# The second half of a matmul stage by Strassen's seven products: 1280 of 2304 tokens of the output projection

## The chip, the cores and the metric

The kernel runs on one core of a Trainium2 chip. The metric is device time in microseconds (us), the time of the slowest core, of which there is one here. The engines are TensorE (PE, and PEld for its weight loads), VectorE (DVE), ScalarE (ACT), GpSimd (POOL, unused) and SyncE (SP, which only issues DMAs). PSUM is the memory that TensorE accumulates in, eight banks of 512 float32 a partition; SBUF is the memory that all engines read.

## The reference

A retention layer feeds a gated layer, and that feeds a layer with a leaky activation; 2304 tokens, float32 in and out (the weights come as float64):

```python
a, b = x @ w1, x @ w2                    # x: 2304 x 512 from the attention
x2 = (a * b @ w3) @ w_out                # 512 wide
h = x2 @ w_in                            # 2304 x 2048
g = np.maximum(h, 0) + alpha * np.minimum(h, 0)
out = g @ w_out2                         # 2304 x 2048 times 2048 x 512
```

Only the last line is touched.

## The kernel before

Every product is made from float32 values cut in two: a high part (a cast to fp32r, on ScalarE) and a low part (value minus high part, on VectorE). A product is three passes: high by high, high by low, low by high. So each operand has to be cut before TensorE can read it.

The stages follow one another on TensorE: the retention, a times b, a fold of w3 with w_out, y (x2), h (x2 @ w_in), and out. The h stage is already done with Strassen's seven products, on pairs of token blocks; its g goes to DRAM in tiles of 128 rows x 384 tokens (`gd[c, b]`).

The out stage (line 970) is a list of 48 steps (line 878): for each of six blocks of W = 384 tokens, eight steps j; a step takes two of the 16 chunks of 128 rows of w_out2 (`wbc[2j]`, `wbc[2j+1]`, each high and low). The first 16 steps alternate between blocks 0 and 1, for w_out2 is still being converted from float64 then; after that each block has its eight steps in a row. A step issues 3 chunks of tokens x 2 chunks of rows x 3 passes = 18 matmuls with 512 columns; g is the stationary operand, w_out2 the moving one. Each chunk of 128 tokens has a PSUM bank, which is copied and written out after its step j = 7 (`write`).

Three steps ahead SP loads g (`load_g`, tiles `gr`, three buffers), one step ahead ScalarE and VectorE cut it (`split_g`, tiles `gh` and `gl`, two buffers). The conversion of w_out2 (`Weights`, a step of it at each tick) takes VectorE's time in the early steps.

TensorE, ScalarE and SP run their instructions in the order of the code. VectorE's order is set by a scheduler when the program is built; on the chip each of the four engines works off its own list in order.

Of the kernel before, what the change touches and what calls it, by code (L numbers as in the profile page):

```python
# [7 lines left out]
F32 = mybir.dt.float32  # L8
# [24 lines left out]
def _f32(ap):  # L33
    return ap.bitcast(F32)
# [103 lines left out]
def retention_moe_kernel(ctx: ExitStack, tc, qk, kv, w_out1, w3t, w12, w_in, w_out2, alpha, c_row, c_pair, out):  # L138
    nc = tc.nc

    def pool(stack, name, bufs=1, **kw):
        return stack.enter_context(tc.tile_pool(name=name, bufs=bufs, **kw))
# [634 lines left out]
    py.close()  # L777


    back = pool(ctx, "back", side="right", reuse_waits="tile")  # L780
    pg = ExitStack()
    gp = pool(pg, "gp", side="right", bufs=2, reuse_waits="tile")

    def fetch(q, u):
# [90 lines left out]
            self.from_sum(self.b3, self.u2, 0, 1)  # L875

    NM = W // P
    steps = [(j, b) for j in range(C1) for b in range(2)] + [(j, b) for b in range(2, NB) for j in range(C1)]
    loaded, ready, accs = {}, {}, {}

    def load_g(n):
        if n < len(steps):
            j, b = steps[n]
            t = loaded[n] = gr.tile([P, 2, W], F32, tag="gr", name=f"gr{n}")
            for m in range(2):
                nc.sync.dma_start(out=t[:, m], in_=gd[2 * j + m, b])

    def split_g(n):
        if n < len(steps):
            x = loaded.pop(n)  # L890
            ready[n] = tuple(ghl.tile([P, 2, W], F32R, tag=f"g{m}", name=f"g{m}{n}") for m in "hl")
            split(ready[n][0], ready[n][1], x)

    def write(b, i):
# [70 lines left out]
    flush()  # L965


    pg.close()
    used = 0
    for n, (j, b) in enumerate(steps):  # L970
        if ws.at[3] < len(ws.pieces):
            ws.tick()
            ws.until(n_in + 2 * j + 2)
        load_g(n + 3)
        split_g(n + 1)
        if b not in accs:
            accs[b] = [bank((used + i) % 8, f"o{b}_{i}") for i in range(NM)]
            used += NM
        h, l = ready.pop(n)
        for i in range(NM):  # L980
            ic = slice(i * P, (i + 1) * P)
            for m in range(2):
                wh, wl = wbc[2 * j + m]
                for q, (x, y) in enumerate(((h, wh), (h, wl), (l, wh))):
                    nc.tensor.matmul(accs[b][i], x[:, m, ic], y, start=(j == 0 and m == 0 and q == 0),  # L985
                                     stop=(j == C1 - 1 and m == 1 and q == 2))
            if j == C1 - 1:
                write(b, i)


# [79 lines left out]
```

## Time and profile before

| | us |
|---|---|
| median of 3 runs (lowest to highest) | 812.07 (811.72 to 814.09) |
| the profiled execution | 812.48 |
| its span, from the first to the last instruction | 810.7 |
| TensorE busy | 793.1 |
| VectorE busy | 499.6 |
| ScalarE busy | 349.7 |

The mean granted clock of TensorE is 0.992 of 2.4 GHz. In rows of a timeline a name such as `o<-wb,gh` is the tile written and those read; "[3.12 <-PE o]" says that the engine sat idle for 3.12 us and that TensorE's write of o ended it. Matmuls overlap in the pipeline, so their spacing is read from their starts and not from their durations. DMA issues have a row on SP's queue (SPq).

### The profile page before, as it was taken

The page shows a single profiled execution, that of the slowest core. Times are in us where ns is not written, and L with a number is a line of the kernel's source. Part 1 is how long each engine was busy: PE and PEld are TensorE (multiplying, and loading weights), DVE is VectorE, ACT ScalarE, POOL GpSimd, SP SyncE. Part 2 cuts the span into 40 slices and gives each one's busy share as a digit, 9 for nine tenths or more (in the row PEclk, how much of TensorE's full clock was granted, in tenths as well). Part 3 has the DMA queues.
Part 4 walks back from the last instruction along what each step waited for, and adds up shares of the span by engine and source line. Part 5 has one row for each costly group of instructions (what it writes and reads, how often), then busy time and mean ns, then how long its engine had stood idle before and what let it go on. Part 6 is the DMA issues. An engine that isn't in the chain of part 4 may idle for free.

```text
span 810.7 us, 12667 instructions
## 1 busy us (share of the span) xinstructions
PE 793.1 (98%) x4768; PEld 699.9 (86%) x4768; DVE 499.6 (62%) x895; ACT 349.7 (43%) x648; POOL 0.2 (0%) x4
## 2 busy tenths in 40 slices
PE   7989999999999999999999999999999999999998
PEld 4768888888888988999999999999997888888886
DVE  4786776325467789979752568677889923222222
ACT  3452562232245566655534455455566622222221
POOL 0000000000000000000000000000000000000000
PEclk8989999999999999999999999999999999999999
DMA  9845821371076658999934935325566735344341
GB/s 348 300 142 200 303 112 78 105 280 79 27 229 181 213 184 300 308 375 402 394 129 151 380 116 186 127 98 186 172 212 223 238 98 175 97 138 137 98 135 40
DMA packets 78845, 155.91 MB, mean 192 GB/s; under 512 B 7872, under 2 KB 55488, under 8 KB 78784
## 3 DMA queue, kind: packets, MB, share of 16 engines
q1 hardware_dynamic: 78784, 155.10, 54.5%
q8 instruction: 37, 0.61, 0.3%
q14 instruction: 24, 0.20, 0.1%
HBM read 103.69 MB, written 51.38 MB: 191 GB/s over the span
## 4 chain that ended last, share of the span: by engine, by line
PE 92%; DMA 3%; ACT 2%; DVE 1%; SPq 1%; issue 0%; ACTq 0%
PE ps L179 24%; PE o L985 23%; PE h L824 21%; PE y L757 12%; PE pw L571 5%; PE o L320 2%; DMA kv<-in_kv_dram 2%; PE sc L274 2%; PE o L312 1%; DMA gr<-gd 1%; PE st L288 1%; DVE xs L327 0%; ACT xh L172 0%; PE sc L264 0%; DVE gl L173 0%
## 5 line engine op out<-in xcount | busy, mean ns | idle before, releaser
L179 PE MATMUL ps<-xh,w 128*128 128x512 f32 (+1 forms) x640 | 187.5, 374 | 1.8 <-ACT w L112 1.7
L985 PE MATMUL o<-wb,gh 128*128 128x512 f32 x576 | 177.6, 389 | 1.2 <-ACT gh L172 1.2
L179 PEld LDWEIGHTS ps<-xh,w 128*128 128x128 f32 x640 | 116.9, 190 | 23.7 <-ACT w L112 1.9
L985 PEld LDWEIGHTS o<-wb,gh 128*128 128x128 f32 x576 | 108.0, 188 | 24.0 <-ACT gh L172 1.7
L179 PE MATMUL ps<-xl,w 128*128 128x512 f32 (+1 forms) x320 | 118.8, 371 | 0.0
L985 PE MATMUL o<-wb,gl 128*128 128x512 f32 x288 | 112.3, 390 | 0.5 <-DVE gl L173 0.5
L173 DVE TENSOR_TENSOR gl<-gr,gh 128x768 fp32r<-128x768 f32 x48 | 45.9, 957 | 100.2 <-ACT gh L172 100.0
L757 PE MATMUL y<-yab,wp 128*128 128x384 f32 x576 | 100.0, 334 | 0.0
L757 PEld LDWEIGHTS y<-yab,wp 128*128 128x128 f32 x576 | 99.9, 188 | 0.1
L172 ACT CAST gh<-gr 128x768 fp32r<-128x768 f32 x48 | 40.2, 839 | 116.2 <-PE o L985 111.3
L179 PEld LDWEIGHTS ps<-xl,w 128*128 128x128 f32 x320 | 60.9, 190 | 10.0 <-DVE xl L173 0.3
L985 PEld LDWEIGHTS o<-wb,gl 128*128 128x128 f32 x288 | 54.0, 188 | 12.4 <-DVE gl L173 1.3
L836 DVE SCALAR_TENSOR_TENSOR g<-m,al,g 128x384 f32<-128x384 f32 x48 | 29.7, 618 | 48.2 <-ACT g L835 47.9
L824 PE MATMUL h<-xT,wv 128*128 128x384 f32 x288 | 54.9, 334 | 1.4 <-DVE g L842 1.4
L824 PE MATMUL h<-xT,wu 128*128 128x384 f32 x288 | 55.0, 335 | 0.3 <-ACT h L849 0.3
L108 DVE CUSTOM_DVE_ANT_0 a<-a,b 128x1024 uint16<-128x1024 uint16 x72 | 49.5, 687 | 3.8 <-DVE a L106 0.5
L824 PEld LDWEIGHTS h<-xT,wv 128*128 128x128 f32 x288 | 50.3, 188 | 1.8 <-DVE g L842 1.8
L824 PEld LDWEIGHTS h<-xT,wu 128*128 128x128 f32 x288 | 50.3, 188 | 0.9 <-ACT h L849 0.6
L433 ACT CAST ab<-f 128x512 fp32r<-128x512 f32 (+1 forms) x40 | 23.1, 576 | 64.2 <-DVE f L437 59.8
L437 DVE TENSOR_TENSOR f<-f,ps 128x512 f32<-128x512 f32 (+1 forms) x40 | 25.3, 632 | 35.3 <-PE ps L179 35.0
L103 DVE TENSOR_SCALAR a<-a 128x512 f32<-128x512 f32 x72 | 30.4, 422 | 22.2 <-ACT a L93 21.9
L571 PE MATMUL pw<-wo,w 128*128 128x512 f32 x192 | 43.7, 389 | 0.0
(82 smaller groups left out, 1012.9 us busy)
## 6 DMA issues: line engine op xcount, KB each, us to landing
gd<-g SPq DMA_DIRECT2D x96, 192.0 KB, 1.9
gr<-gd SPq DMA_DIRECT2D x96, 192.0 KB, 2.5
abd<-ab SPq DMA_DIRECT2D x32, 512.0 KB, 3.7
raw<-in_w_out_dram SPq DMA_DIRECT2D x24, 512.0 KB, 4.0
qk<-in_qk_dram SPq DMA_DIRECT2D x16, 576.0 KB, 7.1
yab<-abd SPq DMA_DIRECT2D x24, 384.0 KB, 8.5
kv<-in_kv_dram SPq DMA_DIRECT2D x16, 544.0 KB, 7.9
raw<-in_w_dram SPq DMA_DIRECT2D x16, 512.0 KB, 7.4
```

The costliest lines, as they stand in the source:

```text
L103: nc.vector.tensor_scalar(out=a, in0=a, scalar1=self.LEAST, scalar2=self.MOST, op0=ALU.max, op1=ALU.min)
L108: nc.vector.tensor_tensor(out=a.bitcast(I32), in0=a.bitcast(I32), in1=b, op=ALU.add)
L172: nc.scalar.copy(hi, src)
L173: nc.vector.tensor_tensor(out=lo, in0=src, in1=_f32(hi), op=ALU.subtract)
L179: nc.tensor.matmul(ps, a, bb, start=(n == 0), stop=(n == last))
L433: nc.scalar.copy(t[:, 0], f)
L437: nc.vector.tensor_tensor(out=f, in0=f, in1=pss[1], op=ALU.mult)
L571: nc.tensor.matmul(acc[i], a[:, ic], bb, start=(k == 0 and n == 0), stop=(k == C1 - 1 and n == 2))
L757: nc.tensor.matmul(ys[o], wpc[c][a][:, oc], yab[b, c][:, bb], start=(c == 0 and i == 0), stop=(c == C1 - 1 and i == 2))
L824: nc.tensor.matmul(ps, a[:, x, ks], b[:, y, k], start=(fresh and n == 0), stop=(n == 5), skip_group_check=True)
L836: nc.vector.scalar_tensor_tensor(out=g, in0=r, scalar=neg[:, c:c + 1], in1=g, op0=ALU.mult, op1=ALU.add)
L985: nc.tensor.matmul(accs[b][i], x[:, m, ic], y, start=(j == 0 and m == 0 and q == 0), stop=(j == C1 - 1 and m == 1 and q == 2))
```

## The change

Blocks 0 and 1 (384 tokens) and the first 256 tokens of block 2 stay as they were: 24 steps, the last eight of them with 12 matmuls instead of 18. The other 1280 tokens are five groups of 256. For such a group g, as a matrix of two halves of tokens by two chunks of rows, is multiplied with the 2 x 2 blocks of two chunks of w_out2 (128 rows x 256 columns each) by seven products instead of eight, in the form with 15 sums. A tail step is one j of one group: seven products x three passes = 21 matmuls with 256 columns, into four banks (`q`) that hold two halves each; eight steps make a group.

What is new around it:
- `t_sums`, `rest`: for each j the sums of w_out2's blocks. w0 and w1 add high and low part again, t12 and t34 hold the four sums; `t123` and `t4` take their high parts (ScalarE) and low parts (VectorE). Sixteen pieces; one is issued at each plain step once the conversion of w_out2 is through, what is left after the last plain step.
- `load_two`, `add_two`: for two steps eight loads of 128 x 128 of g into a tile `gs` (three buffers) and four sums of it on VectorE.
- `high_part`, `low_part`: the seven operands of a step cut in two in one instruction each (128 x 896), tiles `go` (three buffers); `high_part(n + 2)` and `low_part(n + 1)` are issued at step n.
- after the last step of a group the four banks are added up on VectorE (one copy on ScalarE) and written with two DMAs.
- the room of `back` (tiles of w_in's operands) is closed before the out stage and used for `gs` and `go`.

```diff
-    steps = [(j, b) for j in range(C1) for b in range(2)] + [(j, b) for b in range(2, NB) for j in range(C1)]
+    PLAIN = ((0, W), (1, W), (2, 256))
+    steps = [(j, *x) for j in range(C1) for x in PLAIN[:2]] + [(j, *PLAIN[2]) for j in range(C1)]
...
+    gs = pool(ctx, "gs", side="right", bufs=3, reuse_waits="tile")
+    go = pool(ctx, "go", side="right", bufs=3, reuse_waits="tile")
...
+        for m, w in enumerate((w0, w1)):
+            h, l = wbc[2 * j + m]
+            nc.vector.tensor_tensor(out=w, in0=_f32(h), in1=_f32(l), op=ALU.add)
+        less(t12[:, :HW], w0[:, HW:], w0[:, :HW])
+        less(t12[:, HW:], w1[:, HW:], t12[:, :HW])
+
+        def rest():
+            t34 = tmp.tile([P, DM], I32, tag="b", name=f"t34_{j}", bufs=2).bitcast(F32)
+            less(t34[:, :HW], w1[:, HW:], w0[:, HW:])
+            less(t34[:, HW:], w1[:, :HW], t12[:, HW:])
...
+            for t, cols, src in places:
+                nc.scalar.copy(t[:, 0, cols], src)
+            for t, cols, src in places:
+                nc.vector.tensor_tensor(out=t[:, 1, cols], in0=src, in1=_f32(t[:, 0, cols]), op=ALU.subtract)
...
+    def load_two(u):
...
+        t = sums_of[u] = gs.tile([P, 2, 7, P], F32, tag="gs", name=f"gs{u}")
+        t0 = T0 + 2 * u // C1 * 256
+        for i in range(2):
+            j = (2 * u + i) % C1
+            for m in range(2):
+                for h in range(2):
+                    b, at = divmod(t0 + h * P, W)
+                    nc.sync.dma_start(out=t[:, i, PLACE[f"A{h + 1}{m + 1}"]],
+                                      in_=gd[2 * j + m, b][:, at:at + P])
...
+        for out, x, y, how in (("S1", "A21", "A22", ALU.add), ("S3", "A11", "A21", ALU.subtract),
+                               ("S2", "S1", "A11", ALU.subtract), ("S4", "A12", "S2", ALU.subtract)):
+            nc.vector.tensor_tensor(out=a[out], in0=a[x], in1=a[y], op=how)
...
+    PRODUCTS = (("A11", "B11", 0, 0), ("S2", "T2", 0, 1), ("S3", "T3", 1, 0), ("S1", "T1", 2, 1), ("A22", "T4", 2, 0),
+                ("A12", "B21", 3, 0), ("S4", "B22", 3, 1))
+
+    ahead = [lambda: load_two(0), lambda: load_two(1), lambda: load_two(2), lambda: add_two(0), lambda: add_two(1),
+             lambda: high_part(0), lambda: (low_part(0), high_part(1))]
...
-    for n, (j, b) in enumerate(steps):
+    for n, (j, b, w) in enumerate(steps):
         if ws.at[3] < len(ws.pieces):
             ws.tick()
             ws.until(n_in + 2 * j + 2)
+        else:
+            t_steps.tick(1)
         load_g(n + 3)
         split_g(n + 1)
+        if n >= len(steps) - len(ahead):
+            ahead.pop(0)()
...
+    t_steps.rest()
+
+    for n in range(n_tail):
...
+        high_part(n + 2)
+        low_part(n + 1)
+        if n % 2:
+            add_two(n // 2 + 2)
+            load_two(n // 2 + 3)
+        x = gops.pop(n)
+        for a, op, k, half in PRODUCTS:
...
+            for i, (y, z) in enumerate(((0, 0), (0, 1), (1, 0))):
+                nc.tensor.matmul(ps, a[:, y], b[z], start=(opens and j == 0 and i == 0),
+                                 stop=(j == C1 - 1 and i == 2), skip_group_check=True)
...
+            elif op == "B22":
+                nc.vector.tensor_tensor(out=ot[:, :DM], in0=e, in1=four[3], op=ALU.add)
+                nc.sync.dma_start(out=out[t0:t0 + P, :], in_=ot[:, :DM])
```

How the engines' lists move is not in the diff. On VectorE, in the kernel before, the place where block 2 ends (gl21 to gl25 are low parts of g for the 22nd to the 26th step, ot2 the copies of finished banks) reads:

```order
L173 TENSOR_TENSOR gl21_7105<-gr21_7051,gh21_7104 128x768
L173 TENSOR_TENSOR gl22_7130<-gr22_7076,gh22_7129 128x768
L173 TENSOR_TENSOR gl23_7155<-gr23_7101,gh23_7154 128x768
L173 TENSOR_TENSOR gl24_7180<-gr24_7126,gh24_7179 128x768
L899 COPY ot2_0_7189<-o2_0_7005 128x512
L899 COPY ot2_2_7207<-o2_2_7007 128x512
L173 TENSOR_TENSOR gl25_7214<-gr25_7151,gh25_7213 128x768
```

There VectorE had one low part a step. In the changed kernel the rows that follow the last plain step's (gs3 are sums of g for the seventh and eighth tail step, t12_7 and t34_7 the last sums of w_out2, go2 the operands of the third tail step) read:

```order
L1042 TENSOR_TENSOR gs3_7367<-gs3_7367 128x2x128
L986 TENSOR_TENSOR t12_7_7317<-w0_7_7315 128x256
L986 TENSOR_TENSOR t34_7_7322<-w1_7_7316,w0_7_7315 128x256
L1042 TENSOR_TENSOR gs3_7367<-gs3_7367 128x2x128
L986 TENSOR_TENSOR t12_7_7317<-w1_7_7316,t12_7_7317 128x256
L1042 TENSOR_TENSOR gs3_7367<-gs3_7367 128x2x128
L986 TENSOR_TENSOR t34_7_7322<-w1_7_7316,t12_7_7317 128x256
L1042 TENSOR_TENSOR gs3_7367<-gs3_7367 128x2x128
L1007 TENSOR_TENSOR t123_7_7325<-t12_7_7317,t123_7_7325 128x512
L1007 TENSOR_TENSOR t123_7_7325<-t34_7_7322,t123_7_7325 128x256
L1007 TENSOR_TENSOR t4_6_7308<-t34_7_7322,t4_6_7308 128x256
L1052 TENSOR_TENSOR go2_7336<-gs1_7114,go2_7336 128x896
```

So the low part of the third tail step stands behind all the sums of w_out2 and behind sums of g for four tail steps later.

ScalarE in the kernel before, about the same place:

```order
L172 CAST gh23_7154<-gr23_7101 128x768
L172 CAST gh24_7179<-gr24_7126 128x768
L897 COPY ot2_1_7198<-o2_1_7006 128x512
L172 CAST gh25_7213<-gr25_7151 128x768
L172 CAST gh26_7241<-gr26_7176 128x768
```

And in the changed kernel, from the high part of the second tail step (go1) past the copy of the last plain bank (ot2_1) to the high part of the third (go2):

```order
L1047 CAST go1_7267<-gs0_7075 128x896
L899 COPY ot2_1_7284<-o2_1_7048 128x512
L1005 CAST t123_5_7290<-t12_5_7261 128x512
L1005 CAST t123_5_7290<-t34_5_7287 128x256
L1005 CAST t4_4_7234<-t34_5_7287 128x256
L1005 CAST t123_6_7307<-t12_6_7299 128x512
L1005 CAST t123_6_7307<-t34_6_7304 128x256
L1005 CAST t4_6_7308<-t34_6_7304 128x256
L1005 CAST t123_7_7325<-t12_7_7317 128x512
L1005 CAST t123_7_7325<-t34_7_7322 128x256
L1005 CAST t4_6_7308<-t34_7_7322 128x256
L1047 CAST go2_7336<-gs1_7114 128x896
```

Nine casts for the last three sets of sums have come between, and each set's source is written on VectorE after the casts of the set before it.

## Rows read from the trace of the kernel before

**Rows 1.** The page: TensorE's busy share, and the chain that ended last.
```profile
PE 793.1 (98%) x4768; PEld 699.9 (86%) x4768; DVE 499.6 (62%) x895; ACT 349.7 (43%) x648; POOL 0.2 (0%) x4
...
PE 92%; DMA 3%; ACT 2%; DVE 1%; SPq 1%; issue 0%; ACTq 0%
```

**Rows 2.** Table by stretches: width, busy time (instructions) by engine, granted clock, DMA.
```profile
core 0: us, PE busy (x) PEld busy (x) DVE busy (x) ACT busy (x) POOL busy (x), PEclk, DMA share, GB/s
...
632.00:652.00 20.00, 20.00 (x90) 16.57 (x89) 17.43 (x29) 11.36 (x19) 0.00 (x0) 1.00 0.64 211
652.00:676.00 24.00, 24.00 (x108) 19.87 (x107) 8.20 (x10) 6.34 (x9) 0.00 (x0) 1.00 0.36 115
676.00:700.00 24.00, 24.00 (x108) 19.87 (x107) 6.39 (x7) 5.03 (x6) 0.00 (x0) 1.00 0.44 139
...
265.00:287.00 22.00, 22.00 (x185) 22.00 (x185) 15.57 (x33) 10.86 (x25) 0.00 (x0) 1.00 0.57 178
```

**Rows 3.** TensorE in order of time, 512 columns: start, duration, what, how many.
```profile
699.70 0.39 PE L985 MATMUL o<-wb,gl 128*128 128x512 f32 x1
...
702.42 0.39 PE L985 MATMUL o<-wb,gl 128*128 128x512 f32 x1
```

**Rows 4.** TensorE in order of time, 256 columns, first and last of 36 triples.
```profile
274.67 0.28 PE L179 MATMUL ps<-xl,w 128*128 128x256 f32 x1
...
287.27 0.28 PE L179 MATMUL ps<-xl,w 128*128 128x256 f32 x1
```

**Rows 5.** Groups of instructions by shape: count, busy us, mean ns, idle before.
```profile
L173 DVE TENSOR_TENSOR gl<-gr,gh 128x768 fp32r<-128x768 f32 x48 | 45.9, 957 | 100.2 <-ACT gh L172 100.0
...
L172 ACT CAST gh<-gr 128x768 fp32r<-128x768 f32 x48 | 40.2, 839 | 116.2 <-PE o L985 111.3 <-DMA gr<-gd 4.9
...
L112 ACT CAST wb<-a 128x512 fp32r<-128x512 f32 x16 | 9.9, 619 | 3.2 <-DVE a L108 3.2
```

**Rows 6.** VectorE in order of time, in an earlier stage: operations back to back.
```profile
345.60 0.69 DVE L661 TENSOR_TENSOR wu<-a,wu 128x512 fp32r<-128x512 f32 x1
346.20 0.42 DVE L665 TENSOR_TENSOR s<-a 128x256 f32<-128x256 f32 x1
346.53 0.42 DVE L667 TENSOR_TENSOR s<-a,a 128x256 f32<-128x256 f32 x1
346.87 0.42 DVE L666 TENSOR_TENSOR s<-s,a 128x256 f32<-128x256 f32 x1
347.32 0.42 DVE L668 TENSOR_TENSOR s<-a,s 128x256 f32<-128x256 f32 x1
```

**Rows 7.** ScalarE in order of time, at the end of the sixteenth step.
```profile
675.01 0.59 ACT L897 COPY ot<-o 128x512 f32<-128x512 f32 x1 [2.15 <-PE o L985]
676.10 0.84 ACT L172 CAST gh<-gr 128x768 fp32r<-128x768 f32 x1 [0.50 <-PE o L985]
```

**Rows 8.** Table by stretches, TensorE alone: width, busy, granted clock, DMA.
```profile
43.00:44.00 1.00, 0.77 (x4) 0.65 0.10 33
...
50.00:51.00 1.00, 1.00 (x7) 0.94 0.92 373
```

**Rows 9.** TensorE in order of time about its idle pieces.
```profile
43.23 0.87 PE L288 MATMUL st<-kv 128*64 128x64 f32 x4 [0.97 <-ACT kv L253]
45.76 0.80 PE L179 MATMUL ps<-xh,w 128*128 128x512 f32 x1 [1.66 <-ACT w L112]
46.36 0.63 PE L179 MATMUL ps<-xl,w 128*128 128x512 f32 x1
46.78 0.63 PE L179 MATMUL ps<-xh,w 128*128 128x512 f32 x1
```

**Rows 10.** SP's queue in order of time: eight loads of 192 KB.
```profile
496.62 3.64 SPq L938 DMA_DIRECT2D xs<-x2d  x8
```

**Rows 11.** The tile gr from 640 to 700: its loads of 192 KB.
```profile
DMA to landing us min/median/max: 2.3/2.5/3.4
```

**Rows 12.** All engines in order of time, the end: the last copy.
```profile
806.88 0.69 DVE L899 COPY ot<-o 128x512 f32<-128x512 f32 x1 [2.03 <-PE o L985]
```

More of the change, by code (lines that the diff above doesn't have):

```diff
@@ L777, in retention_moe_kernel @@
     py.close()
-    back = pool(ctx, "back", side="right", reuse_waits="tile")
     pg = ExitStack()
+    back = pool(pg, "back", side="right", reuse_waits="tile")
     gp = pool(pg, "gp", side="right", bufs=2, reuse_waits="tile")
@@ L882, in load_g @@
         if n < len(steps):
-            j, b = steps[n]
-            t = loaded[n] = gr.tile([P, 2, W], F32, tag="gr", name=f"gr{n}")
+            j, b, w = steps[n]
+            t = loaded[n] = gr.tile([P, 2, W], F32, tag="gr", name=f"gr{n}")[:, :, :w]
             for m in range(2):
-                nc.sync.dma_start(out=t[:, m], in_=gd[2 * j + m, b])
+                nc.sync.dma_start(out=t[:, m], in_=gd[2 * j + m, b][:, :w])
     def split_g(n):
@@ L890, in split_g @@
             x = loaded.pop(n)
-            ready[n] = tuple(ghl.tile([P, 2, W], F32R, tag=f"g{m}", name=f"g{m}{n}") for m in "hl")
+            w = steps[n][2]
+            ready[n] = tuple(ghl.tile([P, 2, W], F32R, tag=f"g{m}", name=f"g{m}{n}")[:, :, :w] for m in "hl")
             split(ready[n][0], ready[n][1], x)
@@ L968, in retention_moe_kernel, with t_sums, less @@
     pg.close()
+    gs = pool(ctx, "gs", side="right", bufs=3, reuse_waits="tile")
+    go = pool(ctx, "go", side="right", bufs=3, reuse_waits="tile")
+    HW = DM // 2
+    T0 = sum(w for _, w in PLAIN)
+    n_tail = (NT - T0) // 256 * C1
+    t123, t4, sums_of, summed, gops = {}, {}, {}, {}, {}
+    def t_sums(j):
+        w0, w1 = (tmp.tile([P, DM], F32, tag="a", name=f"w{m}_{j}", bufs=3) for m in range(2))
+        t12 = tmp.tile([P, DM], I32, tag="b", name=f"t12_{j}", bufs=2).bitcast(F32)
+        def less(out, a, b):
+            nc.vector.tensor_tensor(out=out, in0=a, in1=b, op=ALU.subtract)
+        for m, w in enumerate((w0, w1)):
[7 more added lines that the diff above has]
+            less(t34[:, HW:], w1[:, :HW], t12[:, HW:])
+            t123[j] = xo.tile([P, 2, 2, W], F32R, tag="xo", name=f"t123_{j}").rearrange("p a b w -> p a (b w)")
+            if j % 2 == 0:
+                t4[j // 2] = in_wa(2 + j // 2, f"t4_{j}")
+            at = slice(j % 2 * HW, (j % 2 + 1) * HW)
+            places = ((t123[j], slice(0, DM), t12), (t123[j], slice(DM, DM + HW), t34[:, :HW]),
+                      (t4[j // 2], at, t34[:, HW:]))
+            for t, cols, src in places:
+                nc.scalar.copy(t[:, 0, cols], src)
+            for t, cols, src in places:
+                nc.vector.tensor_tensor(out=t[:, 1, cols], in0=src, in1=_f32(t[:, 0, cols]), op=ALU.subtract)
+        return rest
@@ new lines, in add_two, with high_part @@
+    def add_two(u):
+        if 2 * u >= n_tail:
+            return
+        t = sums_of[u]
+        a = {op: t[:, :, n] for op, n in PLACE.items()}
+        for out, x, y, how in (("S1", "A21", "A22", ALU.add), ("S3", "A11", "A21", ALU.subtract),
+                               ("S2", "S1", "A11", ALU.subtract), ("S4", "A12", "S2", ALU.subtract)):
+            nc.vector.tensor_tensor(out=a[out], in0=a[x], in1=a[y], op=how)
+    def high_part(n):
+        if n < n_tail:
+            x = gops[n] = go.tile([P, 2, 7, P], F32R, tag="go", name=f"go{n}")
+            nc.scalar.copy(x[:, 0], sums_of[n // 2][:, n % 2])
```

47 lines of the change are left out of this document (44 added, 3 removed).

## The prediction

> **What bounds the kernel now.** I read the page's busy shares first, then the table by stages, then the order of time on each engine around the place that the change touches. TensorE is busy for 793.1 of 810.7 us and the chain that ended last is TensorE for 92% [rows 1]. In the stretches of the last product (the g times w_out2 stage) TensorE is busy from end to end, from 632 on without a gap, at a granted clock of 1.00, while VectorE falls from 17.43 of 20 us to 8.20 and 6.39 of 24 us [rows 2]. So in this stage the number of matmuls times their spacing is the time, and VectorE and ScalarE are covered as long as they deliver in time. The reader is to see two things: what a matmul costs by its width, and how much room VectorE has just before the place where the new tail begins.
>
> **The change, part by part.** *Matmuls.* 1280 tokens are 10 chunks of 128; each took 16 rows of w_out2 times 3 passes, 480 matmuls of 512 columns. In their place stand 40 steps of 7 products times 3 passes, 840 matmuls of 256 columns: the same width in total times 7/8. The spacing is what counts. At 512 columns two starts four triples apart lie 702.42 - 699.70 = 2.72 us apart, so 0.2267 us for one [rows 3]. At 256 columns, with a weight load for each as here, starts 35 triples apart lie 287.27 - 274.67 = 12.60 us apart, 0.120 us for one [rows 4]. It is not half of 0.2267; about 13 ns come with every matmul. 480 x 0.2267 = 108.8 us goes, 840 x 0.120 = 100.8 us comes: **-8.0 us**, not the 13.6 us that an eighth of 108.8 would be.
>
> In the 256-column stretch the weight loads fill the time too, 22.00 of 22.00 us [rows 2]. The Trainium skill, "TensorE: Matmul & The Clock Gate", section "Back-to-back issue gap", speaks against such a change: it gives pairs of load and matmul a spacing of about 81 ns at 128 columns and 131 ns at 512, so that halving the width saves far less than half of the time. Between its two figures 256 columns would be some 98 ns (an estimate from that page), and 840 x 98 against 480 x 131 ns would be 19 us more, where the rows give 8 us less. The rows differ from both its figures and from its ratio, and they decide.
>
> *VectorE before the tail.* This is where the change costs. The eight sets of sums of w_out2 take, each, two additions of 512, four subtractions of 256, and low parts of 512, 256 and 256: nothing of it was there before. The sums of g add four operations of 256 for every two tail steps, and each tail step a low part of 896. Durations: 512 elements 0.69 us, 256 elements 0.42 us, 768 elements 957 ns [rows 5, 6]; 896 is not shown and is 1.09 us by the slope between 512 and 768 (an estimate). Back to back they start closer than they last: 0.61 us after a 512, 0.335 after a 256, and 0.455 after a 256 on whose result the next one rests [rows 6]; so 1.0 us after an 896. An addition on 128x2x128 is not in the trace; between the 0.42 us of 256 elements in a row and the 0.69 us of 512 I take the former.
>
> In the order as built, VectorE's 82 instructions from the first low part of the sums of rows 2 and 3 of w_out2 (t123_1) to the low part of the tail's third step (go2) stand in one row, with the last plain steps' own work among them: 25 of 512 elements, 54 of 256 (16 of these on 128x2x128), 3 of 896. That is 25 x 0.61 + 54 x 0.335 + 3 x 1.0 = 36.4 us. The first needs ScalarE's cast of the same sums, and that stands on ScalarE behind the copy of a finished bank, which starts at 675.01 [rows 7]: 0.59 us of copy and 0.62 us of cast [rows 5], which overlap by 0.1 us as neighbours on an engine do, make 676.1. The spare time of VectorE before that, 15.8 of the 24 us to 676 [rows 2], can only take the first set and the additions of the next two: in ScalarE's order the casts of each set stand behind the cast of a later step's g or such a copy. With 0.6 us for dependent pairs and casts on ScalarE the low part of the third step is there at 676.1 + 36.4 + 0.6 = **713.1**.
>
> When does TensorE want it? The step after 676.1 is the seventeenth [rows 7]; eight plain steps of 12 matmuls are 8 x 12 x 0.2267 = 21.8 us, so the tail begins at 697.9, its third step 2 x 21 x 0.120 = 5.0 us later, and the third matmul of that, the first that reads a low part, at 703.1. TensorE is late by 713.1 - 703.1 = **+10.0 us**. Some 2.3 us of it should fall in the last three plain steps, whose low parts of g stand in the same row, the rest in one gap ahead of the third tail step. ScalarE is no way round it: there the high part of the third step stands behind nine casts of sums, which wait for VectorE one set after the other. Bounds: with the start at 675.5 and nothing dependent 8.7 us; with each instruction at its full duration (25 x 0.69 + 54 x 0.42 + 3 x 1.09 = 43.2 us) 16.2 us. I take 10.0, since the closer spacing is what rows 6 show for the same kinds of operation.
>
> *Clock.* A gap of that length is followed by slow matmuls: in a stretch with idle pieces of 0.97 and 1.66 us and little work between them the granted clock fell below 1 between 43 and 44, to its lower level (1.2 GHz), and was back soon after 50, some 4.3 us after steady work began at 45.76 [rows 8, 9]. Matmuls of 512 start 46.78 - 46.36 = 0.42 us apart there, so 256 columns are some 0.213 us (an estimate, the half); 4.3 us hold 20 of them, each 0.093 us late: **+1.9 us**. Bounds 0 (the clock stays, or the loads below would have held TensorE anyway) and 2.6 (6 us of it).
>
> *Tail.* In 2.52 us a step asks 0.95 us of ScalarE (839 ns of 768 elements and the slope), and of VectorE 1.0 + 0.8 us, and 2.4 us more once in eight steps: less than it has. On SP two loads of 192 KB a step become eight of 64 KB every two steps. Eight in a row took 3.64 us to issue, and one lands 2.3 us after its issue at the least, 2.5 in the middle, 3.4 at the most [rows 10, 11]; 3.2 + 2.3 = 5.5 us against 5.04 us of TensorE, with three tiles in turn. I put it at 0 and take it up as a rival. The tiles' room (closing `back` earlier) costs nothing: its last readers are matmuls of the stage before, which ended long before the first load of g for the tail. The four banks of a tail group alternate with four others, so draining one is covered by the next group, except at the end.
>
> *End.* Before, one copy of 0.69 us stood between the last matmul and the last write [rows 12]. Now the last addition of 512 stands behind another that became possible six matmuls (0.72 us) before the end and has a chain of three ahead of it. Between -0.1 and +1.1 us; **+0.4**.
>
> Sum: -8.0 + 10.0 + 1.9 + 0.4 = +4.3 us. The profiled execution took 812.48 us (810.7 of span and 1.8 around it), so 816.8; it lay 0.4 over the median of 812.07, so the forecast is **816.4 us**.
>
> **The rivals.** *VectorE is covered.* Then the matmuls' 8.0 us come through: 812.1 - 8.0 + 0.4 = 804.5. For it: two stretches of 24 us with only 8.20 and 6.39 us of VectorE [rows 2], 33 us free of 48, what the eight sets need at 4.1 us each. Against: the order puts nearly all of them after 676, where 21.8 us are left. Faster than before begins where the third low part comes earlier than 710.6, 2.5 us before my count.
>
> *The loads of g pace the tail.* Slower than the forecast. The first sum of a new pair of steps stands on VectorE ahead of a low part that TensorE wants soon, and it can only run when loads have landed that were issued after an older low part freed their tile. Low part, 5.5 us of loads, a sum of 0.335, the low part of 1.0: 6.9 us, where two tail steps give 5.04 (twice, early in the tail) and later three give 7.56. At 2.3 us of landing that costs two times 1.8 us at most, which the slow clock's 1.9 us partly hides; at the 3.4 us that rows 11 show as the most, 8.0 against 7.56 us, it binds about every third step: 13 x 0.4 and 2 x 2.9, 11 us. So 818 to 827.
>
> *No change.* The sum's low ends together, 8.7 us late, no slow clock, +0.2: 812.1 + 0.9 = 813.0. The slow clock needs the gap to be in one piece; if it is spread over the plain steps, which share the queue, it goes.
>
> *Weight loads aren't hidden.* If the loads set the spacing, 840 matmuls could take as long as those of 512 columns do, 840 x 0.2267 = 190 us, +82 instead of -8: up to 902. Rows 4 show 0.120 with loads of the same shape, and the table 185 matmuls in 22.00 us [rows 2]. The page named above stands for this case. That the products are not computed as said can be excluded: the order as built has 840 matmuls of 128x256 at the new line.
>
> **How the numbers follow.** Forecast 0.62 (its own range 814 to 820), loads 0.15, no change 0.16, covered 0.06, weight loads 0.01. A difference under 0.3% (2.4 us) can't be told from no change here: the three runs shown spread over 2.4 us. Faster needs 809.6, only the covered case: 0.06. Within: the no-change case and a little of the forecast's low end, 0.17. Slower 0.77. The range goes from 812.0, which takes in most of the no-change case, to 822.5, the half of the loads' case; left out are the covered case, a third of the loads' and a little of no change.
>
> **What would show it.** In the profile after, matmuls of 256 columns 0.36 us for three at clock 1.00; VectorE busy without a gap from about 676 to 713; one gap of TensorE of 6 to 8 us about 5 us into the tail, released by ScalarE's high part or VectorE's low part of go; a granted clock of 0.5 for some 4 us behind it; short waits for the low parts of g in the last plain steps. Wrong would be: no such gap (VectorE covered), many short waits for go through the whole tail with VectorE idle on loads of gs (the loads), or another spacing than 0.12.

## The result, and the profile after

The changed kernel takes 820.09 us (median of 4 runs, 818.34 to 822.17); the kernel before, run beside it, 811.89 us (4 runs, 811.29 to 814.09). The ratio is 1.0092, 95% interval 1.0072 to 1.0112: slower by 8.2 us. The forecast was 816.4 us with a range of 812.0 to 822.5. The profiled execution took 821.37 us, its span is 819.6 us, 8.9 us above that of before.

The page first: busy times, the chain that ended last, and the groups of the new matmuls (count | busy us, mean ns | idle before them).

```profile
PE 790.1 (96%) x5128; PEld 712.5 (87%) x5128; DVE 580.9 (71%) x1081; ACT 372.0 (45%) x690; POOL 0.2 (0%) x4
...
PE 70%; DMA 10%; DVE 8%; SPq 7%; issue 3%; ACT 2%; DVEq 0%; ACTq 0%
...
L1107 PE MATMUL q<-t,go 128*128 128x256 f32 x480 | 65.2, 286 | 0.0
...
L1107 PE MATMUL q<-wb,go 128*128 128x256 f32 x360 | 52.9, 289 | 8.7 <-ACT go L1047 6.7
```

Against [rows 1] TensorE is busy for 3.0 us less and VectorE for 81 us more. TensorE's share of the chain fell from 92 to 70%. One idle piece of 6.7 us stands out in the last row. The table by stages shows where (columns as in [rows 2]):

```profile
652.00:676.00 24.00, 24.00 (x107) 19.87 (x107) 15.22 (x26) 7.06 (x11) 0.00 (x0) 1.00 0.31 104
676.00:700.00 24.00, 22.57 (x97) 17.50 (x96) 22.42 (x52) 11.13 (x22) 0.00 (x0) 1.00 0.56 163
700.00:720.00 20.00, 12.94 (x82) 12.14 (x81) 16.18 (x33) 7.97 (x15) 0.00 (x0) 0.83 0.26 77
...
720.00:740.00 20.00, 20.00 (x167) 19.92 (x167) 14.64 (x25) 7.55 (x9) 0.00 (x0) 1.00 0.29 86
```

VectorE has 9 us free before 676, is then full, and while it is, TensorE stands: 82 matmuls between 700 and 720 where 167 fit. From 720 on 167 matmuls take 20.00 us, 0.120 us each. The Trainium skill, "TensorE: Matmul & The Clock Gate", section "Back-to-back issue gap", gives 81 ns at 128 columns and 131 ns at 512; here it is 120 ns at 256 and 227 ns at 512 [rows 3], and the 19 us more that its figures would make by the prediction's estimate did not come.

VectorE's row, its first and its last instruction: the first low part of the sums of rows 2 and 3 of w_out2, and the low parts of go2 to go4.

```profile
677.46 0.69 DVE L1007 TENSOR_TENSOR t<-t,t 128x512 fp32r<-128x512 f32 x1 [1.85 <-ACT t L1005]
...
713.52 3.08 DVE L1052 TENSOR_TENSOR go<-gs,go 128x896 fp32r<-128x896 f32 x3
```

TensorE in order of time, at its waits and behind the long one:

```profile
623.74 0.73 PE L1084 MATMUL o<-wb,gh 128*128 128x512 f32 x2 [2.40 <-ACT gh L172]
...
698.49 0.73 PE L1084 MATMUL o<-wb,gh 128*128 128x512 f32 x2 [1.43 <-ACT gh L172]
...
713.48 0.80 PE L1107 MATMUL q<-wb,go 128*128 128x256 f32 x2 [6.68 <-ACT go L1047]
714.66 0.58 PE L1107 MATMUL q<-wb,go 128*128 128x256 f32 x1 [0.38 <-DVE go L1052]
715.04 2.76 PE L1107 MATMUL q<-t,go 128*128 128x256 f32 x12
717.60 1.67 PE L1107 MATMUL q<-wb,go 128*128 128x256 f32 x9
719.11 1.60 PE L1107 MATMUL q<-t,go 128*128 128x256 f32 x12
```

Three things are to be seen. The third tail step starts 6.7 us late, released by ScalarE's high part of go, and its third matmul waits for VectorE's low part, as forecast. From 714.66 to 719.11 stand 22 matmuls, which is 4.45 us instead of 2.64. And there is a wait that the forecast did not have, at 698.49, for the last plain step's g. The wait at 623.74 stands in the kernel before too, but is shorter there:

```profile
622.41 0.73 PE L985 MATMUL o<-wb,gh 128*128 128x512 f32 x2 [1.23 <-ACT gh L172]
```

The granted clock of after about the third tail step (TensorE alone: width, busy, clock, DMA):

```profile
712.00:713.00 1.00, 0.00 (x0) 0.50 0.00 0
...
718.00:719.00 1.00, 1.00 (x9) 0.71 0.51 139
719.00:720.00 1.00, 1.00 (x11) 1.00 0.58 137
```

The clock fell to its lower level (1.2 GHz) while TensorE stood idle, and it rose again between 718 and 719. The mean of 0.71 there puts the rise at some 718.6 (an estimate), 5.1 us after work began at 713.48.

The end, in answer to [rows 12]: the last addition, behind one that could start six matmuls earlier.

```profile
815.15 0.68 DVE L1121 TENSOR_TENSOR ot<-u,q 128x512 f32<-128x512 f32 x1
815.75 0.68 DVE L1126 TENSOR_TENSOR ot<-e,q 128x512 f32<-128x512 f32 x1
```

I count by the *stage*: from the matmul of h after an idle 1.45 us at about 606, found in every profile here, to the end of the span. Before it is 810.7 - 606.03 = 204.7 us, after 819.6 - 606.20 = 213.4 us. The *tail's excess* is the time from the first to the last of the 840 matmuls less 839 x 0.12 = 100.7 us: 12.7 us after.

### The profile page after: what moved, and what is told of

It is laid out like the page before. It is cut to its first block, busy times and chain, and to the rows that moved or that the text cites. A ratio compares the mean times of both kernels' runs of the same rounds, so it can differ in the third digit from the quotient of the medians.

```text
span 819.6 us, 13832 instructions
## 1 busy us (share of the span) xinstructions
PE 790.1 (96%) x5128; PEld 712.5 (87%) x5128; DVE 580.9 (71%) x1081; ACT 372.0 (45%) x690; POOL 0.2 (0%) x4
## 4 chain that ended last, share of the span: by engine, by line
PE 70%; DMA 10%; DVE 8%; SPq 7%; issue 3%; ACT 2%; DVEq 0%; ACTq 0%
PE ps L179 21%; PE h L824 21%; PE y L757 12%; PE o L1084 7%; SPq L1032 6%; DMA gs<-gd 3%; DMA abd<-ab 2%; PE o L320 2%; DMA kv<-in_kv_dram 2%; PE sc L274 2%; PE q L1107 2%; PE o L312 1%; DMA gr<-gd 1%; DMA raw<-in_w3t_dram 1%; DVE go L1052 1%
## 5 line engine op out<-in xcount | busy, mean ns | idle before, releaser
L1084 PE MATMUL o<-wb,gh 128*128 128x512 f32 x256 | 79.1, 390 | 3.8 <-ACT gh L172 3.8
L1107 PE MATMUL q<-t,go 128*128 128x256 f32 x480 | 65.2, 286 | 0.0
L1047 ACT CAST go<-gs 128x896 fp32r<-128x896 f32 x40 | 36.3, 940 | 60.8 <-PE q L1107 25.1
L1107 PEld LDWEIGHTS q<-t,go 128*128 128x128 f32 x480 | 61.6, 195 | 0.0
L1107 PE MATMUL q<-wb,go 128*128 128x256 f32 x360 | 52.9, 289 | 8.7 <-ACT go L1047 6.7
L1084 PEld LDWEIGHTS o<-wb,gh 128*128 128x128 f32 x256 | 47.8, 188 | 14.4 <-ACT gh L172 4.7
L1107 PEld LDWEIGHTS q<-wb,go 128*128 128x128 f32 x360 | 47.7, 195 | 10.4 <-ACT go L1047 7.2
L1084 PE MATMUL o<-wb,gl 128*128 128x512 f32 x128 | 50.4, 394 | 0.4 <-DVE gl L173 0.4
```

The source lines that it names most:

```text
L1047: nc.scalar.copy(x[:, 0], sums_of[n // 2][:, n % 2])
L1107: nc.tensor.matmul(ps, a[:, y], b[z], start=(opens and j == 0 and i == 0), stop=(j == C1 - 1 and i == 2), skip_group_check=True)
```

## The experiments

All were timed in five rounds beside the kernel before.

| run | median us (runs) | before | ratio, 95% | stage us | tail's excess us |
|---|---|---|---|---|---|
| early_sums | 812.04 (12) | 813.69 | 0.9983, 0.9966 to 1.0001 | 202.6 | 2.0 |
| spread_sums | 812.48 (12) | 813.69 | 0.9985, 0.9973 to 0.9997 | 205.3 | 3.5 |
| no_w_sums | 808.34 (6) | 813.69 | 0.9945, 0.9923 to 0.9967 | 200.8 | 1.3 |
| junk_in_gap | 817.48 (7) | 813.69 | 1.0051, 1.0034 to 1.0069 | 211.1 | 9.5 |
| after_again | 820.22 (5) | 811.13 | 1.0101, 1.0079 to 1.0123 | 213.6 | 12.5 |
| early_sums_loads | 814.40 (12) | 811.13 | 1.0029, 1.0013 to 1.0046 | 205.6 | 1.9 |
| early_sums_tail | 812.23 (12) | 811.13 | 1.0003, 0.9985 to 1.0021 | 205.1 | 2.8 |
| early_sums_pool | 819.64 (5) | 811.13 | 1.0092, 1.0069 to 1.0114 | 210.4 | 1.4 |
| early_sums_order | 808.02 (5) | 813.60 | 0.9932, 0.9919 to 0.9944 | 201.8 | 2.3 |
| early_sums_order_merge | 810.64 (8) | 813.60 | 0.9967, 0.9948 to 0.9986 | 201.3 | 2.4 |
| early_sums_order_copies | 809.22 (5) | 813.60 | 0.9941, 0.9929 to 0.9953 | 202.7 | 1.8 |
| order_only | 820.06 (6) | 811.94 | 1.0090, 1.0069 to 1.0111 | 213.8 | 14.7 |

**The same sums, earlier.** Theory: VectorE's work is not too much, it comes too late. Rival: it is too much wherever it stands, or the loads of g pace the tail.

```diff
-        else:
-            t_steps.tick(1)
+        if n >= 10:
+            t_steps.tick(1.5 if n < 16 else 1)
```

> The sums of w_out2 are issued from the eleventh plain step on (before: from the fourteenth), three pieces for two steps at first, so that all 16 are issued before the tail and none stands between the last plain step and the third tail step. Theory (VectorE's row of 36 us is what made it slower): the gap of 6.7 us, the 0.4 behind it, the 1.4 in the last plain step and the 2.4 of slow clock go, 820.1 - 10.9 = 809.2; the waits for loads of g, partly covered by the slow clock so far, may come to 1 to 2 more: 808.5 to 811.5. Rival (the tail is slow by itself, by its loads and its narrow matmuls): stays at 816 or more, with many short waits for go.

The long gap and the slow clock behind it are gone; the stage is 10.8 us shorter than after, the tail's excess 2.0 instead of 12.7 us. Its table by stages:

```profile
652.00:676.00 24.00, 24.00 (x108) 19.87 (x107) 23.45 (x48) 10.53 (x21) 0.00 (x0) 1.00 0.34 111
676.00:700.00 24.00, 21.61 (x93) 16.84 (x92) 23.06 (x52) 9.85 (x20) 0.00 (x0) 1.00 0.48 142
700.00:720.00 20.00, 20.00 (x168) 19.96 (x168) 13.67 (x22) 8.28 (x10) 0.00 (x0) 1.00 0.45 133
```

VectorE does the same work (581.1 us in the whole run, 580.9 after), now in the free time before 676. But of the 8.0 us that the matmuls save only 2.1 arrive (202.6 against 204.7): the tail has 2.0 us of excess, and TensorE still waits in the plain steps:

```profile
679.45 0.50 PE L1084 MATMUL o<-wb,gl 128*128 128x512 f32 x1 [1.11 <-DVE gl L173]
...
696.91 0.73 PE L1084 MATMUL o<-wb,gh 128*128 128x512 f32 x2 [1.28 <-ACT gh L172]
```

**The same sums, later.** What is left after the plain steps is given one piece a tail step, instead of all at once (`t_steps.rest()`).

```diff
-    t_steps.rest()
...
     for n in range(n_tail):
...
+        t_steps.tick(1)
```

> The pieces of the sums of w_out2 that were left after the last plain step are issued one a tail step, in the order of need; VectorE's work is the same and no earlier. Theory: the low part of the third tail step is there in time, but by the eighth tail step VectorE has the 36.1 us from 677.5 and 8.2 us of other low parts and sums of g behind it, 721.7 against 719.3 when TensorE is there: 2.5 us late in small pieces, no gap of 6.7 us, no slow clock: 820.1 - 6.7 - 0.4 - 2.4 + 2.5 = 813. Rival (the tail is slow by itself): 816 or more.

The stage is 8.1 us shorter than after, with short waits in place of the gap. So what is lost in the kernel after lies in the five pieces that are left then (eleven of the sixteen have been issued at plain steps) and that stand ahead of one low part, not in the amount. The gain would be larger but for the wait at 623: in this execution the clock fell to 0.50 behind it, and the place cost 4.7 us against 3.2 in the profile of after.

**No sums of w_out2.** The seven products read blocks of w_out2 in place of the sums; `t_sums` is left out. The output is another one, so the run tells of time alone.

> Leaves out all sums of w_out2 and their cuts (t_sums): the products that take T1 to T4 read blocks of w_out2 itself instead, so the number, width and order of the matmuls is the same and the output is another. Theory: as with the sums issued early, 808 to 811; what it lies below that run is what the sums still cost there. Rival (the tail is slow by itself): 816 or more.

The stage is 12.6 us shorter than after and 3.9 shorter than before (5.4 by the medians); so the change is worth 4 to 5 us and not 8 even with this load taken off VectorE. What stays are the waits at 623 (2.36 us, before 1.23), at 697 (0.79, and 1.3 us lost with the matmuls beside it), in the tail (1.3) and 0.3 at the end.

**The clock alone.** Thirty matmuls that nobody reads fill the gap, so that TensorE has work and the wait stays.

```diff
+        if n == 2:
+            junk = bank(4, "junk")
+            for _ in range(30):
+                nc.tensor.matmul(junk, wbc[0][0][:, 0:P], wbc[0][0], start=True, stop=True)
```

> 30 matmuls of 512 columns on a bank that nobody reads stand ahead of the third tail step, 30 x 0.227 = 6.8 us, as long as the gap, so that TensorE doesn't idle there. Theory (the slow clock after the gap costs 2.4 us): the granted clock stays at 1.00 and the time falls by 1 to 2.4 us, to 817.7 to 819, since loads of g then bind a little more. Rival (the half-rate stretch was covered by the loads of g anyway): 820.1 within 0.5.

```profile
707.55 6.99 PE L1103 MATMUL junk<-wb 128*128 128x512 f32 x30
...
715.52 0.38 PE L1111 MATMUL q<-wb,go 128*128 128x256 f32 x1 [0.66 <-DVE go L1052]
715.74 1.60 PE L1111 MATMUL q<-t,go 128*128 128x256 f32 x12
717.18 1.24 PE L1111 MATMUL q<-wb,go 128*128 128x256 f32 x9
```

Twelve matmuls behind the wait take 1.44 us here, 2.56 after; the granted clock stays at 1.00. The stage is 2.3 us shorter. The clock's price in the trace of after is 1.8 us of it; the rest is a balance of other waits: 1.4 us less in the tail behind the third low part (1.7 against 3.1), and 1.0 us more ahead of the tail, where in this execution the clock fell behind the wait at 623 too. This gap costs its length and about 2 us more.

**After once more.**

> The changed kernel as it is, on the chip of the next three, to compare with: 1.0092 of before as in its first runs, 1.007 to 1.011.

The gap is 6.54 us at 712.08, the same instructions around it; the stage 213.6. The wait at 623 is 1.37 us here instead of 2.40, so its length belongs to the execution and not to the change. But here the granted clock fell behind it, to 0.50 from 623 to 626, which it did not in the first profile of the same kernel:

```profile
623.00:624.00 1.00, 1.00 (x4) 0.50 1.02 404
```

**Loads of g for the tail earlier.** In early_sums, with the loads issued five steps sooner:

```diff
-    ahead = [lambda: load_two(0), lambda: load_two(1), lambda: load_two(2), lambda: add_two(0), lambda: add_two(1),
-             lambda: high_part(0), lambda: (low_part(0), high_part(1))]
+    ahead = [lambda: add_two(0), lambda: add_two(1), lambda: high_part(0), lambda: (low_part(0), high_part(1))]
...
+        if 12 <= n < 15:
+            load_two(n - 12)
```

> Sums of w_out2 early, as in the run early_sums, and the first three sets of loads of g for the tail at the 13th to 15th plain step instead of the 18th to 20th, where they stood on SP ahead of the last loads of the plain steps. Theory (the wait of 1.4 to 1.6 us ahead of the last plain step is its g, queued behind those loads): that wait goes, the out stage falls from 202.6 us to 201, ratio to before some 0.996. Rival (VectorE is late there and the load only came last by chance): the wait stays, with VectorE or ScalarE as its end, within 0.5 us of early_sums.

A miss: by the stage 3 us worse than early_sums. The wait at 696 went, and a worse one came at 680:

```profile
679.62 0.41 DVE L1042 TENSOR_TENSOR gs<-gs 128x256 f32<-128x256 f32 x1
...
681.56 1.28 DVE L173 TENSOR_TENSOR gl<-gr,gh 128x512 fp32r<-128x512 f32 x2
```

```profile
680.10 0.73 PE L1085 MATMUL o<-wb,gh 128*128 128x512 f32 x2 [1.87 <-ACT gh L172]
682.29 0.79 PE L1085 MATMUL o<-wb,gl 128*128 128x512 f32 x1 [1.46 <-DVE gl L173]
...
682.00:684.00 2.00, 1.71 (x4) 0.58 0.27 76
```

The scheduler that orders VectorE put the sums of g ahead of the low parts of g that TensorE wanted: eight of them stand between 668 and 680, where early_sums has none. The high part that TensorE waited for at 680 stood on ScalarE behind casts of sums of w_out2 that waited for VectorE in turn. (The last row is the clock between 682 and 684.) A load moved on SP moved VectorE's list too.

**The tail's own costs.** On top of early_sums_loads: two loads of neighbouring tokens in one, a finished group's writes issued behind the next loads of g (these lines are left out below), and the copies of the first blocks' banks that VectorE made, four in the trace, given to ScalarE.

```diff
-        if i % 2:
+        if i % 2 or b < 2:
...
+                b, at = divmod(t0, W)
+                if at + 2 * P <= W:
+                    nc.sync.dma_start(out=t[:, i, 0:7:6] if m == 0 else t[:, i, 1:3],
+                                      in_=gd[2 * j + m, b][:, at:at + 2 * P].rearrange("p (h w) -> p h w", h=2))
+                    continue
```

> As early_sums_loads, and three things for the tail and the plain steps: the loads of two halves of g that lie in one block are one DMA (4 instead of 8 for two steps in three of the five groups), a group's writes are issued on SP only behind the next loads of g, and the copies of the first six finished banks are ScalarE's alone. Theory (what is left over the matmuls' 8 us is waits for loads of g that stand behind other issues on SP, and 1.3 us for VectorE at the 17th and 18th step): the out stage falls by 2 to 3 us more, to 198 to 199, ratio 0.992 to 0.993, and the tail has no wait over 0.3 us. Rival (the loads' own latency binds): as early_sums_loads.

No better than before, and 2.8 us of excess in the tail, all of it in the second and third of the five groups, whose loads were merged: fewer loads alone do not take the waits away. In this execution the wait at 622 was followed by half the clock for some 3.5 us (624 to 627.5), which it was not in before, after or early_sums, with a wait of the same kind:

```profile
622.36 0.73 PE L1090 MATMUL o<-wb,gh 128*128 128x512 f32 x2 [1.40 <-ACT gh L172]
...
624.00:625.00 1.00, 1.00 (x4) 0.53 0.97 379
```

**Additions on GpSimd.** On top of early_sums_tail the sixteen additions of 512 (w0, w1) move from VectorE to GpSimd.

```diff
-            nc.vector.tensor_tensor(out=w, in0=_f32(h), in1=_f32(l), op=ALU.add)
+            nc.gpsimd.tensor_tensor(out=w, in0=_f32(h), in1=_f32(l), op=ALU.add)
```

> As early_sums_tail, and the 16 additions that put high and low part of w_out2 together again are GpSimd's, 9.8 us less on VectorE. Theory: nothing waits for VectorE there any more, so nothing is gained, within 0.5 us of early_sums_tail. Rival (VectorE still paces the last plain steps): 1 us or more faster. Against both: GpSimd is slow enough, or hinders VectorE enough, to make it slower.

A clear loss, 7 us against early_sums_tail. The groups by shape (count | busy us, mean ns | idle before) of the run with GpSimd:

```profile
L990 POOL TENSOR_TENSOR w<-wb 128x512 f32<-128x512 f32 x16 | 27.9, 1752 | 668.9 <-DVE wb L116 649.1 <-DVE t L986 19.8
...
L986 DVE TENSOR_TENSOR t<-w,t 128x256 f32<-128x256 f32 x16 | 12.0, 752 | 1.6 <-POOL w L990 1.4
L1007 DVE TENSOR_TENSOR t<-t,t 128x512 fp32r<-128x512 f32 x8 | 10.8, 1353 | 1.1 <-ACT t L1005 1.1
```

and of early_sums_tail:

```profile
L986 DVE TENSOR_TENSOR t<-w,t 128x256 f32<-128x256 f32 x16 | 6.6, 414 | 0.0
...
L1007 DVE TENSOR_TENSOR t<-t,t 128x512 fp32r<-128x512 f32 x8 | 5.5, 681 | 0.0
```

GpSimd took 1.75 us for what VectorE does in 0.68, and VectorE's own operations beside it went from 414 to 752 and from 681 to 1353 ns: VectorE gave away 10.9 us of additions and was busier in all, 583.7 instead of 578.5 us. The Trainium skill, "GPSIMD Engine Reference", section "8. Key points", says that GpSimd shares its way to SBUF with VectorE and disturbs instructions with two SBUF inputs; the trace agrees, these have two.

**One set of loads behind the plain steps' loads.** In early_sums the loads for tail steps 5 and 6 stand on SP ahead of the last plain step's load of g; SP's queue there, early_sums first (start, time to issue, what, how many):

```profile
688.86 0.85 SPq L887 DMA_DIRECT2D gr<-gd  x2
689.76 3.75 SPq L1032 DMA_DIRECT2D gs<-gd  x8
693.61 0.85 SPq L887 DMA_DIRECT2D gr<-gd  x2
```

```diff
-    ahead = [lambda: load_two(0), lambda: load_two(1), lambda: load_two(2), lambda: add_two(0), lambda: add_two(1),
-             lambda: high_part(0), lambda: (low_part(0), high_part(1))]
+    ahead = [lambda: load_two(0), lambda: load_two(1), lambda: None, lambda: (load_two(2), add_two(0)),
+             lambda: add_two(1), lambda: high_part(0), lambda: (low_part(0), high_part(1))]
```

> early_sums with one thing changed: the third set of eight loads of g for the tail stands on SP behind the loads of g of the last plain step instead of ahead of them. In the kernel after and in early_sums TensorE waited 1.2 to 1.6 us about 695 for the operands of the last plain step. If the eight loads of 64 KB ahead on SP are the reason, that wait is below 0.3 us here, the third and later tail steps wait no more than before, and the stage (from the last gap of the stage before to the end of the span) is 202.6 - 1.4 = 201.2 us. If VectorE's row (100% busy from 676 to 692 in early_sums) is the reason, the wait stays at 1.2 or more, with VectorE's low part of g as the releaser, and the stage stays at 202.6. A third way: the later loads make the fifth tail step wait, 1 to 2 us about 708, and the stage gains nothing.

```profile
689.75 1.81 SPq L887 DMA_DIRECT2D gr<-gd  x4
691.61 3.76 SPq L1032 DMA_DIRECT2D gs<-gd  x8
```

The last load of g is issued 3 us sooner, the wait at 696 is gone and no other came in its place. 808.02 us, 0.9932 of before: this version beats both kernels. The stage shows 0.8 us against early_sums and 2.9 against before (201.8; the wait at 622 was 0.4 us longer in this execution). The ratio of the medians says 5.6 us against before, 4 more than that of early_sums. The profiled execution of early_sums is its fastest (809.04; others took up to 815.29), the one here lies within 807.80 to 809.40. A part of this goes with the clock: four of the five executions here have a mean granted clock of 0.992 or more, but only five of the twelve of early_sums, and among those alone the medians are 807.9 and 810.1 us. So the edit is worth between 1 and 4 us, and no run here says more exactly how much.

**Two more edits on top**: the merged loads of the tail, and with them the copies of the first blocks' banks on ScalarE (both diffs stand above).

> early_sums_order, and in the tail the two loads of 128 x 128 of neighbouring tokens are one of 128 x 256 wherever they lie in one tile of g (four of the five groups): four loads for two steps on SP instead of eight. In the kernel after TensorE waited 0.3 to 0.8 us at four places of the tail, about 2 us together, where the sum of g on VectorE had waited for loads. If the time that eight loads take to issue (3.7 us) is the reason, four take 1.9 us, the tail's waits fall to 0.5 us or less together, and the stage is 1 to 1.5 us shorter than that of early_sums_order. If the landing or VectorE's order is the reason, they stay at 1.5 to 2 us and the stage is the same within 0.5 us.

> early_sums_order_merge, and the three copies of finished banks of the first two blocks that VectorE made go to ScalarE: 3 x 0.61 = 1.8 us less on VectorE between 668 and 677, where its row delays the low part of g for the first step behind those blocks (TensorE waited 1.3 us at 677.7 in early_sums). If VectorE's row is the reason that wait is below 0.3 us and the stage 1.0 to 1.3 us shorter than that of early_sums_order_merge. If the loads of g are the reason (SP has writes of finished banks ahead of them) it stays at 1.0 to 1.5 us. With all three edits right, the kernel would be 3.5 to 4 us below early_sums, 0.994 of the kernel before.

Neither gains by the medians; by the stage the merged loads are 0.5 us better, and with the copies the clock fell behind the wait at 622, which cost 2 us more there. Two of the five groups, the first and the fourth, don't have their loads merged, for their 256 tokens lie in two tiles of g. (The expectations say four groups of five, and three copies where there are four.) So SP issues 112 loads instead of 160 (the first two rows: what, how many, KB each, us to landing), and the longest wait of the tail comes at its 31st step, in the fourth group:

```profile
gs<-gd SPq DMA_DIRECT2D x64, 64.0 KB, 2.0
gs<-gd SPq DMA_DIRECT2D x48, 128.0 KB, 2.6
...
776.87 0.39 PE L1112 MATMUL q<-wb,go 128*128 128x256 f32 x1 [1.23 <-DVE go L1057]
```

The tail's excess is 2.4 instead of 2.3 us. By groups (from the first matmul of a group to that of the next, less 168 x 0.12 us) it is 0.0, 0.1, 0.6, 0.2 and 1.4 us in early_sums_order, 0.0, 0.0, 0.6, 1.9 and 0.0 with merged loads, and 0.0, 0.0, 0.1, 1.8 and 0.0 with the copies too. The waits went out of the last group, which is merged, and came up in the fourth, which isn't. So these runs neither show nor exclude that the number of loads makes the waits. With the copies moved, the wait at 680 is 0.99 instead of 1.11 us: ScalarE's cast of g then stood behind those copies and casts. The expected 0.994 of before is met (0.9941), but by the order alone.

**The order alone, without the earlier sums.**

> The kernel after with one change alone, that of early_sums_order: the third set of eight loads of g for the tail stands on SP behind the last plain steps' loads of g; the sums of w_out2 stay late. The wait of 1.43 us at 698 before the last plain step should go (below 0.3). If the low part of the third tail step is set by VectorE's row, that row is as long as before and the gap at the third tail step grows by what the earlier wait gave: low part at 36 to 37 us after the row's start, stage 212.5 to 213.5 us, about 820 us, ratio to before 1.008 to 1.010: two edits that are each worth little alone and 12 us together. If the load order has a worth of its own, the stage is 211.5 to 212.0 (818.5 us).

```profile
697.29 0.50 PE L1084 MATMUL o<-wb,gl 128*128 128x512 f32 x1 [1.13 <-DVE gl L173]
...
712.89 0.80 PE L1107 MATMUL q<-wb,go 128*128 128x256 f32 x2 [8.00 <-ACT go L1047]
```

The same edit is worth nothing here. The load's wait at 698 became one of 1.13 us for VectorE's low part (I had expected none), and the gap grew from 6.68 to 8.00 us: the third tail step starts when VectorE's row ends, whenever TensorE arrives (its third matmul comes 108.2 us into the stage, 108.5 after).

## Why the prediction was right, and where it was short

The sign, the place and the mechanism were right; the sum was 4.4 us short of the profile's 8.7. Point by point, with after's times taken 0.17 us earlier for its later start of the stage:

| step | predicted | in the trace of after |
|---|---|---|
| spacing of 256 columns | 0.120 us, -8.0 | 0.120 us (167 in 20.00 us), -8.0 |
| VectorE's row, its length | 37.0 us | 714.66 - 677.46 = 37.2 us |
| VectorE's row, its start | 676.1 | 677.46 - 0.17 = 677.3 |
| third tail step's low part against 703.1 | +10.0 | 714.66 - 0.17 - 703.1 = +11.4 |
| slow clock behind the gap | +1.9 | 4.45 - 2.64 = +1.8 |
| waits for go in the tail behind 719.11 | 0 | 12.7 - 7.8 - 1.8 = +3.1 |
| end | +0.4 | (819.6 - 815.03) - (810.7 - 806.46) = +0.3 |
| sum | +4.3 | +8.6 (stage: +8.7) |

(7.8 is how late the third step's third matmul is against 44 x 0.12 us from the tail's first; 815.03 and 806.46 are the last matmuls' starts.)

*VectorE's row* was the main term, and it came out by counting 82 instructions in the built order with spacings from an earlier stage [rows 6]; its length is off by 0.2 us. A little of that is luck: the 0.6 us added for dependent pairs and casts were 0.55 us of waits in the trace, and 0.43 of them, at 709.56, were for a load of g, which the row was not to wait for. That early_sums and spread_sums give back 10.8 and 8.1 us with the same instructions in other places shows that the order, not the amount, is the cause. The split was less good: 2.3 us of it were to fall in the last plain steps as waits for low parts; there fell one wait of 1.43 us, for a load of g that stands on SP behind three sets of eight loads for the tail. I had looked at that queue for the tail only, not for the plain steps it is shared with. In after this wait costs nothing (order_only), since the gap swallows it; it costs where the gap is gone (early_sums against early_sums_order).

*The start of the row* is 1.2 us late because the wait at 623 was 2.40 us in this execution and 1.23 us in the profile of before. It changes from one execution to the next (1.37 us in after_again, with the same code; 1.21 to 2.40 over the fourteen profiles), so this part is not shown to be the change's.

*The loads of g* are the term that was mis-sized: "I put it at 0 and take it up as a rival." It is 3.1 us. The rival had it at 2 to 11 us and was right that VectorE waits for loads ahead of a low part; its row in the profile of after, and the landing of the loads:

```profile
L1042 DVE TENSOR_TENSOR gs<-gs 128x256 f32<-128x256 f32 x80 | 33.3, 421 | 17.9 <-DMA gs<-gd 17.0
...
DMA to landing us min/median/max: 1.7/2.0/3.9
...
758.69 0.38 PE L1107 MATMUL q<-wb,go 128*128 128x256 f32 x1 [0.35 <-DVE go L1052]
```

Most of the 17.0 us cost TensorE nothing: 7.3 of them, ahead of the sums at 720 and 727, stand soon after the gap, and no wait of TensorE over 0.1 us follows until 746. The load of 3.9 us, issued at 739.26, was followed by a low part that came 0.6 us late, at 748; others of 3.7 us, at 723.58 and 772.69, made no low part late by more than 0.1 us. Two of the waits, at 758.69 and 800.18, 1.4 us of the 3.1 together, come in the third step of a group. There VectorE had waited 0.73 and 1.11 us for a load and then had no idle time up to the late low part, with the five additions of the finished banks (2.2 us by their spacing) among its work. The prediction has those ("2.4 us more once in eight steps: less than it has"), but not together with a wait for a load. The rival's price, by SP's issue time for each pair of steps (3.2 us), is neither shown nor excluded: with 112 loads instead of 160 the waits moved from one group to another. What would remove them, a low part that doesn't stand behind a waiting sum in VectorE's list, wasn't tried. So the rest is shown to be low parts that come late behind waits for loads, and not which property of the loads or of VectorE's list sets their size.

*The clock and the end* came out within 0.1 us in the trace. For the clock junk_in_gap shows the same by itself: with work in the gap no fall there, and 2.3 us less in all. The low clock lasted 5.1 us where 4.3 were forecast, but TensorE waited in it once more, so that the loss came out alike.

*No change* and *VectorE is covered* were excluded by the gap; covered (804.5 forecast) is what early_sums_order comes near to with 808.0 (beside a before of 813.6), the difference being waits at 622 and 680 and in the tail. *Weight loads* were excluded by the spacing of 0.120 us; the 902 of that rival is a slip, for 812.1 + 82 is 894. The row's 36.4 is 36.3 when added up; neither changes the forecast.

## What to carry to other kernels

Fewer products with more sums is a trade between TensorE and the engine that makes the sums: count the sums in the order in which that engine will do them, and find the first low part that TensorE wants behind them; the amount per stage (here VectorE was 9 of 24 us free just before) says nothing of it. Work that has no due time of its own should be given out while that engine is idle, some steps before its reader, and never in a heap ahead of something due. When a long gap is closed, look for the smaller waits that it had swallowed: an edit worth nothing beside the gap (order_only) was worth 1 us by the trace without it, and up to 4 by the medians.

## What the runs showed of the hardware that was not expected

- A gap of TensorE of 6.5 to 8.0 us brought the granted clock to 0.50, and it was 1.00 again 5.0 to 6.1 us after work began (after, after_again, order_only; 1.8 us lost in after).
- The wait at 622 or 623 was followed by a clock of 0.50 in five of the fourteen profiles: after_again (a wait of 1.37 us), early_sums_tail (1.40), early_sums_order_copies (1.68), spread_sums (2.27) and junk_in_gap (2.30). In the others it stayed at 1.00, behind waits of 1.21 to 2.40 us; the longest is that of after. So the length of the wait does not decide it here, and what does is open. Where the clock fell, the matmuls there came 3.7 to 4.7 us later than 0.2267 us apart would make it, the wait included; where it stayed, 2.0 to 3.2.
- The time of an execution goes with its mean granted clock: of the 23 of the kernel before that were timed beside after_again, the 18 at 0.992 or more took 809.7 to 812.3 us and the five below it 813.7 to 815.3. Where in such an execution the clock fell is known for the profiled ones alone.
- With GpSimd's additions of 512 beside them, VectorE's subtractions of 512 took 1353 ns in the mean instead of 681.
- Loads of 128 x 128 (64 KB) took 0.47 us each to issue on SP (8 in 3.75 us) and landed after 1.7 to 3.9 us, 2.0 in the middle; those of 192 KB took 2.3 to 3.4 [rows 11]. A third of the bytes is only half a microsecond sooner.
